# One kernel, its steps in another recorded order

## The chip, the core and the metric

The kernel runs on one core of a Trainium2 chip. TensorE (PE, with its weight loads PEld), VectorE (DVE), ScalarE (ACT) and GpSimd (POOL) each work through their own queue of instructions in order and wait for each other by semaphores; SyncE (SP) issues the DMAs, in order too. TensorE writes to PSUM only, and GpSimd is given SBUF operands alone in this kernel. The metric is the device time of one execution in microseconds.

## The reference

Attention with pooled queries, then a mixer of two layers over tokens and two over channels. B = 4, H = 8, S = 1152, D = 64; after pooling there are 576 queries; the mixer has 256 token units and 1536 channel units.

```python
def _attn_ref(q, k, v):
    q_pool = q.reshape(B, H, S // 2, 2, D).mean(axis=3)
    scores = scale * np.matmul(q_pool, k.transpose(0, 1, 3, 2))
    attn = np.exp(scores - np.max(scores, axis=-1, keepdims=True))
    attn = attn / (np.sum(attn, axis=-1, keepdims=True) + 1e-09)
    return np.matmul(attn, v)

def _moe_ref(x, w_tok1, w_tok2, w_ch1, w_ch2):
    xt = x.transpose(0, 2, 1)
    h = np.maximum(xt @ w_tok1, 0.0) @ w_tok2
    u = x + h.transpose(0, 2, 1)
    return u + np.maximum(u @ w_ch1, 0.0) @ w_ch2
```

q, k and v are float32; the weights are float64 and come as pairs of 32-bit words, which the kernel narrows on the chip (`narrow`, `tok_weights`).

## The kernel before

**Numbers.** A product of float32 is made of fast float32r products: each operand is split into a high part (a cast on ACT) and a low part (a subtraction, on DVE or GpSimd).

**Attention, 32 heads (`main`).** Per head nine steps; each fills one score tile (PSUM, `s`, two of them) with two blocks of 128 keys x 288 queries, by two matmuls each (L967). ACT takes two exponentials from the tile, `pf` (L981) and the high part `ph` (L984). A subtraction makes the low part `pl` (L988, on GpSimd or DVE). TensorE multiplies `ph` and `pl` by the values (L1015) into `o`. There are five `ph` and four `pl` buffers. In 17 heads (`IN_PV`) the values carry a column that gives the row sums, and a step has six such matmuls; in the others it has four, and DVE sums `pf` (L995).

**Ahead of a head.** `load_kq` and `prep_kq` load q and k for two heads, pool the queries (L731, L737), turn and split them. `stack` copies the parts by DMA into one of three sets `kk`, `qq` (L838) and into `k2`, `q2` (L843, L846); a set must have been read for the last time by the head three before. `maxima` multiplies queries by keys once more (L897) into one of three ring banks of PSUM (`r`), from which DVE reduces the row maximum (L899); the maxima go by DMA (L873) into a row of `q2`, so that the score matmul subtracts them.

**Beside it.** In head 1 `tok_weights` narrows the token weights: ACT takes absolute values (L659), GpSimd clamps them (L661, nine times), DVE puts the bits together, with two buffers `w`. After every fourth head `token_mix` runs the token layers for half of the channels (L1113, L1131). `finish` divides by the row sums (L1080 on ACT or L1081 on DVE).

**Channel mixer.** For each block of rows products by `w_ch1` (L1299, 384 columns) and `w_ch2` (L1416, 512 columns). Two thirds of the rows go in pairs, with seven products for eight (`paired`), for which weights are added (L1338) and all are split (L1288 on ACT, L1289 and L1402 on DVE or GpSimd). Sums are taken on DVE (L1370), the activation is split by ACT (L1307) and DVE (L1309). At the end rows of the mixer's input are loaded into one of three buffers (L1428), added (L1434) and stored (L1438, L1442).

**The order.** All this is written down as steps: an engine, the data and buffers it reads and writes, and for some of them a second engine (`other`: by `both` and `either`, and in `finish`). `Plan.run` takes the order of all 7279 steps from the string `ORDER` (differences of step numbers, packed), moves the steps listed in `OTHER` to their second engine, and issues them; a buffer of a pool goes to the step that comes first in this order. So the two tables decide each engine's queue and which buffer a step gets. `DUE` holds numbers that sorted the steps once; it does not change.

```python
order = [self.steps[n] for n in np.cumsum(near.T.copy().view("<i2")[:, 0])]
for n in OTHER:
    self.steps[n].eng, self.steps[n].cost = self.steps[n].other
```

Of the kernel before, what the change touches and what calls it, by code (L numbers as in the profile page):

```python
# [106 lines left out]
class Due(dict):  # L107
# [16 lines left out]
    "i8Sf1{lF*Bo8?fPXw@q}yaJ=+e2_{?3zit}3fxb;?`&yqQ!>+`#kt}Q_Qv)YIy&KW82h4=ATWbLSr>c%A(4sYGiA(qa2h>J}IKe8f*C2N>ms"
    "9bHg_RznZqi3YCXQ)~32|W_POO&lTy?^h9{Cmgsf|uBZ`rHe#uZfOUU$!wq{m|}{x<AZk-"
    ")<$;&>!X!L6Lzvcf$_8o=~SwYAI|*y96wwI)NPJ{#ch}B&(l?CI}(3X;~#^?jOoH7+d4^gG1PB|3ztW<E*PK<45d1gh{e;5|U?KTzBE=ju%s"
    "2Eo+xFY2KZY$ysz7&-"
    "GYzGIzYL!;y$>d^a&a9rd}xyTrog+^mkWpY@MGD%yHZe&NQ4<JD2ZYhh=6Zp|NEa%^_W)`R}u{jUpJG{W}jR)lm~pVSem1x9Pi4MfcWk6ZhS"
    "+SjJfite>6^RCWtt3jFRmbSBxH_l*xZMHQRb&2`<xfz?KWxBra4%~TJHZtONI%-"
    "<Qcb~pSx1_h(tNBT$?Ht37>z+R8eVXgcUBvwRmd%qMu)Q<Sxh&<rY`W^U=CBppU;1%uig4lX0r-q7>!jRI+X5EeJ-"  # L130
    "hZ)AOg=S+VL_a=83v^?2YH41<CshMCb_n__j?mW-JruPCyI8Z$ERn)!Q+A=9nb)_@wR8sl0(54pk;+tsNu<UTDiryS5n(`(XsO`4-u`J-"
    "NTwp+H|WFtujt(@?qems`P|THmWj3kF;opQJIn_QyD_w$Ec?Hwe{)uWTMH<X4*~gy!E^sBc=g{pzk@_QjSHN5uSIGqzeR*%rUVVXjDko^P^|"
    "%Va{efD5}euNB;?6n9iQ>giP4TsEH~mCZT3<hsxzU+z3XFOlzjY?VN-"
    "B|)#rJa2#9=O3ngj{_W=F)1sLar>0^)`5jXCzWkA^G`Dj{}yLB{pG4Cfm51I`OHl2KRfv@nW*oLz|ODsnXX@3<*19-"
    "hFMK&=~$rXnt=%O&vTlv!tb{3bV-bXf0A`My5jt$?W2>>P|28p%`r>PB_8lP%t1GnxqstU4qsz8_zk-8aB#cL0m+o-"
    "`fFN~R<)m6ZbIZto^$Hga7lIFonZ#(o8cesN0r+aUp>ffR)5FcdrkAZO*bEH;T4!BpdlyxT1FnmrVQl5U&R8=wF7*$ZLp)Q2dhMVIs5y~cDq"
    "xi`PB~ns3|M1GFklw6Adr6Iqu<+=@uQl|Mai2{^b*SQCs)7Pkz34^Q@Fj-$r*-"
    "+;_RPE8BVhKYE;co^D3F>tX4nv7CL5y__TVMn%gX=E0KHrIX=3PU9i<e>6w99Qbh-"
    "d**s%OQy%NSZOHXo5SA2Z{v69qIpho;vZd~q*}wy7WtZ2MMm3WCl5cdV(lQOobhrvsb3pbe=?F|CS87IMc^7)8F%58jzKQ#-"
    ";FrFz^wUP#EWpR$GN=wyQjp~KiP@F4HdoK1`o>W#V^YpOY}zbO+4Q<2znJQ%&N!DILNpw%N}{$)tOpm`M4v<a~XTe&9tlYmdy0Zns)bka?q7"  # L140
    "5kJ){q?{Gc61|FD4%=ZeozGw91RN4KjDVbiry{EatxktFu`j11ytZhzB(+=`kU(ScQFTQi`rezOYdb{feS0Y#Ud;m{+9z0@GcTnq7j%;P@fZ"
# [1410 lines left out]
```

## Time and profile before

| | us |
|---|---|
| runs | 857.30, 855.11, 857.35 (median 857.3) |
| profiled execution, span | 855.5 |
| PE busy | 831.3 |
| PEld busy | 770.9 |
| DVE busy | 737.9 |
| ACT busy | 589.4 |
| POOL busy | 508.3 |

The span runs from the first to the last instruction of the one execution that was profiled; it lies 1.8 us below the median of the runs. "Busy" is the time in which an engine had at least one instruction under way; of TensorE it says little, since its matmuls overlap. Attention with the token mixer takes the first 557 us or so, the channel mixer the rest. In rows of groups, the idle time behind the second bar is that of the engine ahead of these instructions, with what ended it.

### The profile page before, as it was taken

What the parts mean: (1) busy time and instruction counts of PE and PEld (TensorE: products, weight loads), DVE (VectorE), ACT (ScalarE), POOL (GpSimd) and SP (SyncE); (2) the same over time, 40 slices, a digit from 0 to 9 for tenths busy, and PEclk for the clock granted to TensorE, in tenths of its full rate; (3) what the DMA queues carried; (4) which work ended last, traced back from release to release, by engine and by line L of the source; (5) the groups of instructions that cost most, each with busy time, mean ns of one, the idle gap of its engine ahead of it and who ended that gap; (6) DMA issues with size and microseconds to landing.
All of it is one profiled execution on the core that took longest, in us unless ns stands there. A gap on an engine that the chain in (4) does not pass through costs nothing.

```text
span 855.5 us, 15871 instructions
## 1 busy us (share of the span) xinstructions
PE 831.3 (97%) x5282; PEld 770.9 (90%) x5282; DVE 737.9 (86%) x1537; ACT 589.4 (69%) x1222; POOL 508.3 (59%) x428
## 2 busy tenths in 40 slices
...
GB/s 185 251 136 141 153 137 152 159 132 148 140 154 149 129 142 161 167 149 154 130 136 141 95 143 86 61 197 173 123 149 38 107 64 24 1 62 86 1 1 112
DMA packets 252195, 104.15 MB, mean 122 GB/s; under 512 B 218640, under 2 KB 233104, under 8 KB 252112
## 3 DMA queue, kind: packets, MB, share of 16 engines
...
q8 instruction: 42, 0.69, 0.4%
...
## 4 chain that ended last, share of the span: by engine, by line
PE 75%; DVE 8%; ACT 5%; DMA 5%; SPq 3%; issue 2%; POOL 1%; DVEq 0%; ACTq 0%; POOLq 0%
PE r L1299 16%; PE o L1015 16%; PE s L967 12%; PE a L1416 11%; PE r L897 7%; PE r L1113 3%; PE r L1416 3%; PE o L1416 3%; PE r L1131 2%; ACT ph L984 2%; ACT pf L981 2%; DVE mx L899 2%; DMA qq<-qh 1%; DVE sum L995 1%; SPq L873 1%
## 5 line engine op out<-in xcount | busy, mean ns | idle before, releaser
L988 POOL TENSOR_TENSOR pl<-pf,ph 128x576 fp32r<-128x576 f32 x248 | 356.7, 1460 | 76.7 <-ACT pf L981 26.5
L981 ACT ACTIVATE pf<-s 128x576 f32<-128x576 f32 x288 | 191.7, 681 | 28.6 <-PE s L967 25.5
L1015 PE MATMUL o<-ph,vv 128*65 128x288 f32 (+2 forms) x882 | 205.5, 302 | 1.5 <-DVE ot L1028 0.8
L984 ACT ACTIVATE ph<-s 128x576 fp32r<-128x576 f32 x288 | 187.3, 658 | 25.6 <-PE s L967 9.4
L899 DVE TENSOR_REDUCE mx<-r 128x1 f32<-128x384 f32 x384 | 192.3, 547 | 14.0 <-PE r L897 11.8
L967 PE MATMUL s<-qq,kk 128*128 128x288 f32 x574 | 171.2, 306 | 4.6 <-ACT ph L984 3.5
L967 PE MATMUL s<-q,k 65*128 65x288 f32 x576 | 167.3, 299 | 0.4 <-DMA k<-kk 0.3
L1015 PE MATMUL o<-pl,vv 128*65 128x288 f32 (+1 forms) x576 | 149.5, 301 | 1.3 <-POOL pl L988 0.7
L1015 PEld LDWEIGHTS o<-ph,vv 128*65 128x65 f32 (+2 forms) x882 | 129.6, 154 | 6.8 <-DVE ot L1028 2.1
L897 PE MATMUL r<-kk,qq 128*128 128x384 f32 x372 | 126.8, 355 | 5.9 <-DMA qq<-qh 1.9
L967 PEld LDWEIGHTS s<-qq,kk 128*128 128x128 f32 x574 | 109.2, 190 | 11.2 <-ACT ph L984 6.7
L1416 PE MATMUL a<-big,h 128*128 128x512 f32 x432 | 113.4, 392 | 0.0
L967 PEld LDWEIGHTS s<-q,k 65*128 65x128 f32 x576 | 109.5, 190 | 0.9 <-issue 0.5
L995 DVE TENSOR_REDUCE sum<-pf 128x96 f32<-128x960 f32 x90 | 101.0, 1133 | 0.0
L1015 PEld LDWEIGHTS o<-pl,vv 128*65 128x65 f32 (+1 forms) x576 | 89.0, 162 | 3.9 <-POOL pl L988 1.0
L1416 PEld LDWEIGHTS a<-big,h 128*128 128x128 f32 x432 | 80.3, 188 | 12.8
L897 PEld LDWEIGHTS r<-kk,qq 128*128 128x128 f32 x372 | 70.1, 191 | 15.4 <-DVE mx L899 4.4
L1299 PE MATMUL r<-ut,wk 128*128 128x384 f32 x276 | 57.1, 339 | 0.0
L1289 POOL TENSOR_TENSOR wk<-wa,wk 128x256 fp32r<-128x256 f32 x19 | 15.0, 793 | 65.0 <-ACT wk L1288 64.9
L1299 PEld LDWEIGHTS r<-ut,wk 128*128 128x128 f32 x276 | 49.6, 188 | 3.1 <-issue 0.2
L1370 DVE TENSOR_TENSOR u<-r,u 128x384 f32<-128x384 f32 x59 | 32.4, 553 | 21.9 <-PE r L1299 20.8
L827 POOL TENSOR_TENSOR vv<-vn,vv 128x576 fp32r<-128x576 f32 x27 | 36.0, 1333 | 8.3 <-ACT vv L824 8.3
...
## 6 DMA issues: line engine op xcount, KB each, us to landing
...
```

Of the source, the lines that this page charges most:

```text
L827: both(NK * D, lambda e: e.tensor_sub(vv[:, :, lo], vn, f(vv)[:, :, hi]), t, ["vn", ("vv", h % 2)], [("vv", h % 2)])
L897: step(PE, mm(SP3), lambda ps=ps, w=w, x=x: te.matmul(at(ps)[:, 0:SP3], w, x, start=True, stop=True), t, read, [ps], [ps])
L899: step(DVE, dve(SP3), lambda ps=ps, m=m: ve.tensor_reduce(m, at(ps)[:, 0:SP3], axis=AX.X, op=ALU.max), t + due["max_of"], [ps], [key])
L967: te.matmul(at(st)[:, i, 0:HF], w[:, c * P:(c + 1) * P], x[:, fq * HF:(fq + 1) * HF], start=(n == 0), stop=(n == len(terms) - 1))
L981: step(ACT, act_ps(2 * HF) + (0 if near else 49), lambda pf=pf, st=st: sc.activation(pf, at(st)[:, :, 0:HF], AF.Exp, scale=ESC), t, [(st, ...
L984: step(ACT, act_ps(2 * HF) + 15, lambda ph=ph, st=st: sc.activation(at(ph), at(st)[:, :, 0:HF], AF.Exp, scale=ESC), t + due["p_hi"], [(st, ...
L988: both(2 * HF, lambda e, pf=pf, ph=ph, pl=pl: e.tensor_sub(at(pl), pf, f(at(ph))), t + due["p_lo"], [("pf", s), ph], [pl], [pl], on=POOL i ...
L995: step(DVE, 65 + 1.06 * (NK + 1) * HF // CUT, lambda fq=fq, cs=cs: ve.tensor_reduce(SUM[:, fq, cs], PF[:, 5 * fq:5 * fq + 5, cs].rearrange ...
L1015: lambda o=o, x=x, w=w, m=m, i=i, c=c, new=new, end=end: te.matmul(at(o)[0:m - w], VV[i2][:, c, w:m], at(x)[:, i], start=new, stop=end),
L1299: te.matmul(at(ps)[:, 0:GT], wb[:, u, c * P:(c + 1) * P], x[v_][:, c], start=(opens and c == 0 and n == 0), stop=(closes and c == H2 - 1 a ...
L1370: step(DVE, dve(GT), lambda: ve.tensor_add(at(out_), at(a)[:, 0:GT], at(b_)), t, [a, b_], [out_], [out_] if get else [])
L1416: te.matmul(at(ps), a[:, x * P:(x + 1) * P], b_, start=(opens and m == 0), stop=(closes and m == 2))
```

## The change

`ORDER` and `OTHER` get other values; nothing else changes. The steps, the work of each, what they depend on and the buffers are the same, 7279 in number. 224 steps change the engine: of the splits of the channel weights (L1289, L1402) 57 go from DVE to GpSimd and 16 the other way, of the weight sums 18 and 9, of the subtractions of `pl` 20 and 13, of the divisions in `finish` 36 from DVE to ACT and 20 back; the rest are smaller. Lines of the changed kernel stand 41 lower (L967 is L926 there, L1015 is L974, L661 is L620, L897 is L856, L1289 is L1248).

```diff
 ORDER = (
-    "c-n1Q1wa*B*PXacNvD9I5{j6Z*npIRhzg?EEnwm^z(B>qeu|<Ppdeu@h=pK_A_5W?-"
...
-OTHER = (20, 216, 218, 434, 435, 436, 437, 438, 619, 620, 621, 623, 632, 768, 769, 770, 772, 923,
+OTHER = (19, 20, 56, 434, 435, 436, 437, 438, 446, 619, 621, 632, 923, 934, 1007, 1480, 1481,
...
```

**TensorE, head 0 into head 1** (during the narrowing of the token weights). `s_82` and `s_83` are the two score tiles, `qq`/`kk` and `q`/`k` the operands of head 1's scores, `vv_119` the values of head 0. Before:

```order
L1015 MATMUL o<-pl_162,vv_119 65x288
L967 MATMUL s_82<-qq_96,kk_91 128x288
L967 MATMUL s_82<-q_99,k_94 128x288
L967 MATMUL s_82<-qq_96,kk_91 128x288
L967 MATMUL s_82<-q_99,k_94 128x288
L1015 MATMUL o<-ph_158,vv_119 64x288
L967 MATMUL s_82<-qq_96,kk_91 128x288
L967 MATMUL s_82<-q_99,k_94 128x288
L967 MATMUL s_82<-qq_96,kk_91 128x288
L967 MATMUL s_82<-q_99,k_94 128x288
L967 MATMUL s_83<-qq_96,kk_91 128x288
L967 MATMUL s_83<-q_99,k_94 128x288
```

and now:

```order
L926 MATMUL s_83<-q_99,k_94 128x288
L974 MATMUL o<-ph_155,vv_119 65x288
L974 MATMUL o<-ph_156,vv_119 64x288
L974 MATMUL o<-ph_155,vv_119 64x288
L974 MATMUL o<-ph_157,vv_119 65x288
L974 MATMUL o<-ph_155,vv_119 65x288
L974 MATMUL o<-pl_161,vv_119 65x288
L974 MATMUL o<-ph_157,vv_119 65x288
L926 MATMUL s_82<-qq_96,kk_91 128x288
L926 MATMUL s_82<-q_99,k_94 128x288
L926 MATMUL s_82<-qq_96,kk_91 128x288
L926 MATMUL s_82<-q_99,k_94 128x288
```

Before, a tile `s_82` is filled, one matmul of values follows, and `s_82` is filled again; now seven matmuls of values stand between the filling of `s_83` and that of `s_82`, and `s_82` was filled last 16 matmuls earlier.

**GpSimd, the clamping of the token weights** (`w_153`, `w_154`; `pl` are the subtractions of heads 0 and 1, `vv_120` the values of head 1). Before, from the first clamping on:

```order
L661 TENSOR_SCALAR w_153<-w_153 128x256
L661 TENSOR_SCALAR w_154<-w_154 128x256
L988 TENSOR_TENSOR pl_162<-pf,ph_156 128x576
L661 TENSOR_SCALAR w_153<-w_153 128x256
L661 TENSOR_SCALAR w_154<-w_154 128x256
L988 TENSOR_TENSOR pl_161<-pf,ph_158 128x576
L661 TENSOR_SCALAR w_153<-w_153 64x256
L661 TENSOR_SCALAR w_154<-w_154 128x288
L988 TENSOR_TENSOR pl_160<-pf,ph_155 128x576
L661 TENSOR_SCALAR w_153<-w_153 128x288
L661 TENSOR_SCALAR w_154<-w_154 128x288
L827 TENSOR_TENSOR vv_120<-vn,vv_120 128x9x64
```

and now:

```order
L620 TENSOR_SCALAR w_153<-w_153 128x256
L620 TENSOR_SCALAR w_154<-w_154 128x256
L620 TENSOR_SCALAR w_153<-w_153 128x256
L620 TENSOR_SCALAR w_154<-w_154 128x256
L947 TENSOR_TENSOR pl_161<-pf,ph_158 128x576
L620 TENSOR_SCALAR w_153<-w_153 64x256
L620 TENSOR_SCALAR w_154<-w_154 128x288
L620 TENSOR_SCALAR w_153<-w_153 128x288
L947 TENSOR_TENSOR pl_162<-pf,ph_159 128x576
L620 TENSOR_SCALAR w_154<-w_154 128x288
L786 TENSOR_TENSOR vv_120<-vn,vv_120 128x9x64
L620 TENSOR_SCALAR w_153<-w_153 128x288
```

The clampings stand closer together: four subtractions and one split of values lie between the first and the ninth before (the ninth is two rows further down), two subtractions and the split now.

**GpSimd, its last twelve instructions**, in the channel mixer (`wk`, `w2h`, `w2l` and `big` hold split weights, `ws` sums of weights, `wa` and `wb` the narrowed weights). Before:

```order
L1289 TENSOR_TENSOR wk_6915<-wa_6906,wk_6915 128x256
L1338 TENSOR_TENSOR ws_6920<-wa_6910 128x256
L1338 TENSOR_TENSOR ws_6921<-ws_6920,wa_6898 128x256
L1338 TENSOR_TENSOR ws_6923<-wa_6898,ws_6921 128x256
L1338 TENSOR_TENSOR ws_6922<-wa_6898,wa_6910 128x256
L1289 TENSOR_TENSOR w2h<-ws_6922,w2h 128x256
L1338 TENSOR_TENSOR ws_6921<-wa_6912 128x256
L1289 TENSOR_TENSOR wk_6915<-wa_6900,wk_6915 128x256
L1289 TENSOR_TENSOR wk_6919<-wa_6910,wk_6919 128x256
L1338 TENSOR_TENSOR ws_6921<-wa_6900,ws_6923 128x256
L1289 TENSOR_TENSOR wk_6914<-wa_6912,wk_6914 128x256
L1402 TENSOR_TENSOR big_71<-wb_6901,big_71 128x512
```

and now:

```order
L1248 TENSOR_TENSOR wk_6928<-wa_6917,wk_6928 128x256
L1361 TENSOR_TENSOR big_71<-wb_6904,big_70 128x512
L1248 TENSOR_TENSOR wk_6925<-wa_6907,wk_6925 128x256
L1248 TENSOR_TENSOR w2h<-ws_6930,w2h 128x256
L1297 TENSOR_TENSOR ws_6931<-wa_6907,ws_6929 128x256
L1297 TENSOR_TENSOR ws_6932<-wa_6909,ws_6930 128x256
L1248 TENSOR_TENSOR wk_6928<-wa_6919,wk_6928 128x256
L1297 TENSOR_TENSOR ws_6929<-wa_6909,wa_6921 128x256
L1248 TENSOR_TENSOR w2l<-ws_6929,w2l 128x256
L1361 TENSOR_TENSOR big_71<-wb_6906,big_70 128x512
L1248 TENSOR_TENSOR w2l<-ws_6931,w2l 128x256
L1361 TENSOR_TENSOR big_71<-wb_6908,big_70 128x512
```

Three splits of 512 columns stand among the last twelve now, where there was one. In the whole queue of GpSimd the splits of 256 columns go from 36 to 65, those of 512 columns from 4 to 16, the weight sums from 23 to 32.

## Rows read from the trace of the kernel before

**Rows 1.** The page, part 1, the engines: busy us, share, count.

```profile
PE 831.3 (97%) x5282; PEld 770.9 (90%) x5282; DVE 737.9 (86%) x1537; ACT 589.4 (69%) x1222; POOL 508.3 (59%) x428
```

**Rows 2.** Busy us per stretch of 20 us: PE, PEld, DVE, ACT, POOL; clock, DMA.

```profile
40.00:60.00 20.00, 16.25 (x74) 12.40 (x73) 18.32 (x44) 12.55 (x30) 19.04 (x17) 0.66 0.66 137
...
100.00:120.00 20.00, 19.64 (x138) 18.36 (x137) 19.68 (x47) 17.75 (x38) 18.34 (x17) 1.00 0.83 150
120.00:140.00 20.00, 19.77 (x148) 19.05 (x148) 19.37 (x40) 18.45 (x38) 19.28 (x15) 1.00 0.69 128
140.00:160.00 20.00, 17.56 (x118) 16.01 (x117) 18.08 (x36) 13.22 (x27) 15.88 (x13) 1.00 0.88 158
...
700.00:720.00 20.00, 20.00 (x102) 18.13 (x101) 14.34 (x26) 9.22 (x22) 9.35 (x11) 1.00 0.19 31
```

**Rows 3.** The chain that ended last: start, us, what, matmuls in it.

```profile
531.55 2.11 PE o L1015 x16
...
557.49 1.05 PE r L1299 x6
...
588.99 2.74 PE a L1416 x12
```

**Rows 4.** Groups by line: count, busy us, mean ns, idle us ahead.

```profile
L967 PE MATMUL s<-qq,kk 128*128 128x288 f32 x574 | 171.2, 306 | 4.6 <-ACT ph L984 3.5 <-ACT pf L981 0.9
...
L1299 PE MATMUL r<-ut,wk 128*128 128x384 f32 x276 | 57.1, 339 | 0.0
```

**Rows 5.** Timeline at 36 to 41 us, ACT and PE: start, us, instruction, [idle before].

```profile
36.34 0.63 ACT L984 ACTIVATE ph<-s 128x576 fp32r<-128x576 f32 x1
...
36.87 0.63 ACT L981 ACTIVATE pf<-s 128x576 f32<-128x576 f32 x1
...
40.08 0.65 ACT L984 ACTIVATE ph<-s 128x576 fp32r<-128x576 f32 x1
...
40.79 0.40 PE L967 MATMUL s<-qq,kk 128*128 128x288 f32 x1 [0.33 <-ACT ph L984]
```

**Rows 6.** Busy us per stretch of 2 us, columns as in rows 2.

```profile
52.00:54.00 2.00, 2.00 (x8) 1.39 (x7) 2.00 (x6) 0.75 (x3) 2.00 (x2) 0.50 0.02 4
...
58.00:60.00 2.00, 2.00 (x14) 1.72 (x13) 2.00 (x5) 0.69 (x2) 2.00 (x2) 1.00 0.62 96
```

**Rows 7.** The chain at 141 to 149 us.

```profile
143.29 5.33 DMA qq<-qh
...
148.75 0.42 PE r L897
```

**Rows 8.** Groups by line of the subtractions on GpSimd and DVE.

```profile
L988 POOL TENSOR_TENSOR pl<-pf,ph 128x576 fp32r<-128x576 f32 x248 | 356.7, 1460 | 76.7 <-ACT pf L981 26.5 <-ACT ph L984 24.3 <-PE o L1015 8.6
...
L1289 DVE TENSOR_TENSOR wk<-wa,wk 128x256 fp32r<-128x256 f32 x35 | 15.7, 456 | 3.3 <-ACT wk L1288 3.1
...
L1289 POOL TENSOR_TENSOR wk<-wa,wk 128x256 fp32r<-128x256 f32 x19 | 15.0, 793 | 65.0 <-ACT wk L1288 64.9
```

**Rows 9.** Timeline of GpSimd and DVE at 819 and 843 us.

```profile
819.23 1.01 POOL L1289 TENSOR_TENSOR wk<-wa,wk 128x256 fp32r<-128x256 f32 x1 [3.51 <-ACT wk L1288]
...
819.56 1.09 DVE L1309 SCALAR_TENSOR_TENSOR h<-u,h 128x384 fp32r<-128x384 f32 x1
...
843.41 0.55 DVE L1309 SCALAR_TENSOR_TENSOR h<-u,h 128x384 fp32r<-128x384 f32 x1
```

**Rows 10.** The chain at the end.

```profile
840.69 2.10 PE a L1416 x9
...
842.81 0.70 DVE u L1434
...
843.53 2.72 DMA out_dram<-u
...
846.63 3.59 DMA u<-mixed
...
851.00 0.69 DVE u L1434
```

More of the change, by code (lines that the diff above doesn't have):

```diff
@@ L124 @@
[L124 to L141, printed above, removed]
@@ new lines @@
+    "&a^9RTl`X`Ji0ZOq`<N&?c-@d)hQ($cP>-sm-T3v!ck0NkQhL4~|IJStRe;CVIu>n6jkX?P|Cq=o%hq@*b<ES4O;FH&NZ?46tvL-g1LwgLv%#b<u"
+    "5wWF9?d!#z$CghKup0xgw;eu;%C6SC{|7<19cU47%TQ!#m`!*`pS{eyY!20*u-C$vys#YOd+SH<%o~Xc9DWRXZjCJ{Jk3$s7&U+H9GV)L>k`iNFG"
+    "#^&Vc(=Du7G_ksGSn*Lg_Z31$@JNu@X3;2bsDCzih*9U%FZ7&v(M0u|JFja(y-d{JC^o2FV}$EkjadT31S*pvY(*CB`G;hjBC}i<@q-6bKP7A_AU"
+    "A5?Tst)V~W3#o-R2@i6Uag5v8bPh+y^{npsu26o^~7YMlGG@*JzDWWOWi!Y+^4<eCqFV^ap5gZ~I#0R4`jRLlC#AWHZeF(5q5V_n5$xBN=VHOSkn"
+    "6nM~<2@5gNQ3Am7X>uCh(5@`tR0PE!TLC?XAt?fCYJjnGB4@2u_Jcxz~p>B!jg9t?Njq>14)1KP0rif?PzxP{U^ZFW&QsgRF)gf9;=_j5bFE!BEz"
```

225 lines of the change are left out of this document (97 added, 128 removed), and 26 rows, old and new, of the table OTHER.

## The prediction

> **What bounds the kernel now.** I read the page first, then busy times by stretch, then the chain and the timelines at the thin places. The page calls TensorE (PE) busy for 97% of 855.5 us [rows 1], which says little, because matmuls overlap and a matmul that is held up counts as busy. So I count work by distance from start to start. Undisturbed stretches of the chain give 0.132 us for a matmul of 288 columns (2.11 for 16), 0.176 for 384 columns (1.05 for 6) and 0.229 for 512 (2.74 for 12) [rows 3].
>
> The attention stage runs until the first product of the channel mixer at 557.5 us [rows 3]. The code issues there 1154 score matmuls and 1458 of probabilities by values, 2612 x 0.132 = 345 us; 432 for the row maxima, 432 x 0.176 = 76 us; 464 of 256 columns in the token mixer, at an estimate of 0.176 x 256/384 = 0.117, 54 us; and transposes and warm-up matmuls, at an estimate of 24 us. That is 499 of 557: some **58 us** of PE's time are lost there. In the channel mixer, 792 x 0.176 + 648 x 0.229 = 288 us of work end at about 850, 293 us after they began; the first microseconds still hold attention work. No product waits [rows 4], and the table shows 20.00 us of 20 [rows 2]. **There is nothing to win behind 560 us, and something to lose.**
>
> Where the 58 us go: at 100 to 120 us PE, VectorE (DVE) and GpSimd (POOL) are all at 18.3 to 19.7 of 20; at 40 to 60 PE is at 16.25 and its granted clock at 0.66 of full, so it stood at the lower of its two levels (1.2 of 2.4 GHz) for a part of it; at 140 to 160 at 17.56 [rows 2]. At 40 to 60 four things meet: the splitting of the token weights loads GpSimd, ScalarE (ACT) and DVE, and the score tiles come too close to each other.
>
> **The change part by part.** No step comes or goes; 224 of those that may run on either of two engines change the engine, and each engine's queue is re-ordered. PE's work is the same, so the time can change only by waits.
>
> *Score tiles.* There are two in PSUM. A tile is free again when ACT has taken both exponentials from it: 0.53 us from the start of the first to the start of the second [rows 5], so about 1.09 for both with what ACT does in between added, plus 0.38 for the tails (matmul 0.306 instead of 0.132 in the mean of its group [rows 4], the exponential 0.65 instead of 0.53, 0.06 from its end at 40.73 to the matmul at 40.79 [rows 5]). For each of 288 re-uses I counted the PE work that stands between the last matmul into a tile and the first of its next tenant. Before, 26 re-uses have too little, by 12.4 us in all; the worst four stand in a row in head 1, with 0.13 to 1.33 us of work where 1.5 to 3.8 are wanted (the first piece shown of PE's order). The trace lost 22.9 us at these 26. After, 20 are short, by 4.2 us, none by over 0.7. Gain: between 0, where another queue is as late, and 22.9 x (1 - 4.2/12.4) = 15.1; at face value 8.2. I take **-10**, between the face value and what was really lost there, nearer to the first because GpSimd is full in this stretch too.
>
> *Banks of the maxima.* The same count for the three ring banks, each freed by DVE's reduction: short at 16 places by 2.7 us before, at 7 by 1.7 after. **-1** (0 to -4).
>
> *GpSimd at the weight split.* From its first subtraction to the ninth clamping of weights (second piece shown) GpSimd has one subtraction of 1.46 us for 576 columns [rows 8] less and one sum of queries of 256 columns less (an estimate of 1.46 x 256/576 = 0.65): 2.1 us. This lies under the same waits as the score tiles and is not added; it is why these can be won at all. If it were not so, the first term would shrink by that much.
>
> *The half clock.* PE's granted clock is 0.50 at 52 to 54, and with PE busy throughout, 8 matmuls start in 2 us; at 58 to 60, at 1.00, there are 14 [rows 6]. Before it fell, PE had waited again and again. The change shortens the waits but does not remove them: **0**, at best -3.
>
> *Keys and queries of the next head.* At 148.75 PE waits for a copy that took 5.33 us from its issue [rows 7], and whose issue had to wait for PE's last reading of the old copy. The PE work between this reading and the first maximum of the new head is 5.4 us before and 5.6 after in this head, so this wait stays. In heads 5, 7, 15 and 31 it falls by 0.8, 1.0, 0.9 and 1.2 us, from 7.4 to 9.8; there it is not the last wait now. SP's queue issues these copies in the order in which they stand, behind loads of q and k. **+1** (0 to +3.9).
>
> *Channel mixer.* GpSimd takes over some 64 steps more than it gives up there (splits L1289 36 to 65, weight sums L1338 23 to 32, splits L1402 4 to 16, L1283 2 to 14); the end of its queue shows it. A split costs 0.79 us there and 0.46 on DVE [rows 8]. What hides that is the lead of the split weights over their products; it is not shown by any row, except that PE never waits. But GpSimd also holds DVE up: a DVE instruction that began at 819.56, 0.33 us into a split on GpSimd, took 1.09 us, and one of the same line at 843.41, with GpSimd done, took 0.55 [rows 9]. I count 16 of this kind in the mixer, from 584.85 to this one, by 0.46 us in the mean; with twice the GpSimd work (my count: 107 us behind 53) they would be 32. DVE gives 27 us of work away and gets 7 us of hold-ups, so it is not the bound. **+1.5** (0 to the rival below).
>
> The Trainium skill, page "SBUF — State Buffer", section "Who interferes with whom", speaks against this part: a DVE instruction with two inputs in SBUF and a GpSimd instruction that reads SBUF exclude each other for the whole instruction. The row of 819.56 agrees (1.09 us instead of 0.55). By that rule every GpSimd step added also takes time from DVE, which is the third case below.
>
> *The tail.* In both, the last three output rows of a block need a load that waits for a store from the same buffer. Before: sum 0.70, store 2.72, 0.38 to the load, load 3.59, and the last sum began at 851.00 [rows 10], 0.7 us after PE, which had 42 matmuls left at 840.7 (42 x 0.229 = 9.6). After, 27 matmuls stand behind the last product, so PE ends 27 x 0.229 = 6.2 us after it. The last load waits for the store of a row that is done 3 products (0.53 us) ahead of that, so it lands 0.2 + 0.70 + 2.72 + 0.38 + 3.59 - 0.53 = 7.1 after it, 0.9 us after PE's end. **+0.2** (-0.5 to +1).
>
> Sum: -10 - 1 + 1 + 1.5 + 0.2 = **-8.3 us**, 855.5 - 8.3 = 847.2 of span. The median of the three runs (857.3) lies 1.8 above the profiled span, so 849.0 beside 857.3.
>
> **The rivals.** *The next queue is as late* (no change). At 100 to 140 us GpSimd is at 18.3 to 19.3 of 20 and DVE at 19.4 to 19.7 [rows 2], and through head 15 the two loads hardly change: my count gives DVE -0.8 us and GpSimd +2.4. Then a score tile freed earlier only waits for GpSimd's subtraction. Left is GpSimd's 2.1 us at the weight split, against it the 1, 1.5 and 0.2 of above: -2.1 + 2.7 = +0.6, so 857.9. Against it speaks that the worst places lie ahead of 60 us, where PE's wait names ACT's exponential [rows 5].
>
> *The mixer starves* (slower). Place: some 60 to 100 us into the channel mixer, where for 40 us of PE's work the new order gives GpSimd 13 us and DVE's steps with both inputs in SBUF 26 us by my count: 39 of 40, if the two exclude each other. Price: 29 splits dearer by 0.79 - 0.46 = 0.33, 9.6 us, and 16 more hold-ups of 0.46, 7.4 us; 17.0 if PE waited for all. It decides once a product stands less than about 1.3 us (0.79 split, 0.46 hold-up) behind the start of its split. With all of it, 849.0 - 1.5 + 17.0 = 864.5; with three quarters, 860. For it: the slack is not visible. Against it: PE does not wait once now, with the same kind of hold-up there [rows 2, 9].
>
> *More than counted*: score tiles at their 15.1, maxima 4, and the clock staying up for 3 gives -21 with the same costs, 838.
>
> **How the numbers follow.** A measurement of this kernel can tell about 0.3% from no change, that is 854.7 to 859.9. Forecast 849 with what lies around it (842 to 854.6): 0.55; more than counted (836 to 842): 0.08; no change: 0.17; the mixer starves: 0.20 (860 to 865). Faster 0.55 + 0.08 = 0.63, same 0.17, slower 0.20. The range leaves out 0.08 below 841 and some 0.10 above 863: 841 to 863. The forecast's own range is 842 to 854.6.
>
> **What would show it.** Right: in the stretch 36 to 56 us the waits of score matmuls for ACT fall below 1 us each, the first product of the channel mixer starts near 547, PE is at 20.00 of 20 behind it, and it ends some 0.9 us before the last sum. Head 9 still waits for its copy by 1 to 2 us. Wrong: the first product still starts at 555 to 558 (then the next queue was as late), or idle time ahead of L1299's counterpart in the mixer (then GpSimd starves it). What I cannot count is many small waits under 0.15 us, about 20 of the 58 us; if the new order makes these larger, the forecast falls without any place to point at.

## The result and the profile after

The changed kernel takes 848.28 us (median of 4 runs, 847.35 to 849.13) beside 857.19 for the one before: a ratio of 0.9907, 95% interval 0.9892 to 0.9922, 8.9 us faster. The profiled execution has a span of 847.4 us. Forecast were 849.0 for the median and 847.2 for the span. The sum was right; of its terms several were not, and they cancelled.

Part 1 of the page after, and busy time by stretch (columns as in [rows 2]):

```profile
PE 827.2 (98%) x5282; PEld 770.5 (91%) x5282; DVE 712.6 (84%) x1445; ACT 591.9 (70%) x1238; POOL 582.7 (69%) x504
```

```profile
40.00:60.00 20.00, 15.63 (x88) 13.22 (x88) 18.38 (x44) 13.39 (x33) 19.06 (x17) 0.83 0.77 157
...
140.00:160.00 20.00, 19.33 (x134) 17.77 (x133) 19.11 (x39) 15.67 (x32) 19.00 (x15) 1.00 0.67 116
...
700.00:720.00 20.00, 20.00 (x100) 17.89 (x99) 12.92 (x24) 7.00 (x16) 9.86 (x12) 1.00 0.20 46
```

GpSimd works 74 us more than before [rows 1], DVE 25 less. At 40 to 60 us GpSimd is as full as before (19.06 against 19.04, [rows 2]) and TensorE's share is no better; what is better is its granted clock, 0.83 of full instead of 0.66, and 88 of its matmuls start there instead of 74. At 140 to 160, where it lost most behind the weight split, TensorE goes from 17.56 to 19.33.

The chain of waits (start, us, what), once at the row that answers to 557.49 in [rows 3], and at the end, where it answers to [rows 10]:

```profile
550.00 1.05 PE r L1258 x6
...
841.21 1.37 PE r L1375 x6
842.58 0.02 issue
842.60 0.69 DVE u L1393
```

So the attention stage gained 557.49 - 550.00 = **7.5 us**. From there to the last sum it was 851.00 - 557.49 = 293.5 before and is 842.60 - 550.00 = 292.6 now, **0.9 less**. What follows the last sum grew by 0.3 (4.5 to 4.8). Together 8.1, the difference of the two spans.

Where in attention, I read by TensorE's own work, which is the same in all kernels here: the distances from start to start of its matmuls, less the pace of each kind (0.132 us for 288 columns, 0.175 for 384, 0.231 for 512, 0.119 for 256, the usual distance of each kind of transpose), summed over stretches of work. "20-40" is the work of the weight split; the first column holds the 1.4 us ahead of the first matmul as well. All kernels of the next sections are in the table; the numbers are us lost:

| | 0-20 | 20-40 | 40-100 | 100-120 | 120-320 | 320-360 | 360-500 | 500-780 | sum |
|---|---|---|---|---|---|---|---|---|---|
| before | 7.2 | 13.7 | 6.1 | 5.2 | 16.0 | 1.8 | 5.7 | 1.2 | 57.0 |
| after | 6.8 | 11.2 | 4.7 | 2.5 | 14.2 | 4.1 | 4.9 | 1.0 | 49.3 |
| head_new | 6.5 | 11.4 | 6.5 | 5.0 | 15.4 | 1.9 | 5.3 | 1.2 | 53.3 |
| head_old | 7.3 | 14.1 | 4.5 | 2.2 | 13.5 | 4.1 | 5.1 | 0.6 | 51.4 |
| mix_old | 6.6 | 10.9 | 5.1 | 2.4 | 14.0 | 3.1 | 4.9 | 1.1 | 48.1 |
| mix_pool | 6.5 | 11.9 | 4.4 | 2.4 | 14.8 | 3.5 | 5.0 | 33.2 | 81.9 |
| x_order | 7.8 | 11.5 | 5.4 | 2.4 | 34.5 | 9.4 | 28.0 | 28.6 | 127.7 |
| x_other | 7.6 | 14.2 | 7.1 | 5.2 | 19.5 | 2.7 | 12.4 | 7.4 | 76.0 |
| pl_back | 6.6 | 11.5 | 7.6 | 2.2 | 29.0 | 8.8 | 19.8 | 1.0 | 86.6 |
| pe_alone | 7.4 | 19.5 | 6.5 | 6.5 | 16.1 | 1.8 | 5.6 | 1.2 | 64.7 |
| v_early | 6.5 | 11.0 | 4.5 | 5.9 | 13.6 | 3.2 | 4.7 | 0.9 | 50.3 |
| copy9 | 7.4 | 14.3 | 5.9 | 10.3 | 16.2 | 1.8 | 5.0 | 1.2 | 62.3 |
| mend | 6.5 | 10.5 | 4.7 | 2.5 | 13.9 | 2.7 | 5.5 | 0.6 | 47.0 |
| mend2 | 6.5 | 11.7 | 5.2 | 2.1 | 14.0 | 1.9 | 5.5 | 0.6 | 47.5 |

Only 2.9 us of the gain lie in the first 40 us of work, though the four worst re-uses of score tiles are there; 4.1 lie at 40 to 120; and at 320 to 360 the new order loses 2.3 more than the old one (1.5, if a wait of 0.7 us that stands right at the border of 320 in the kernel before is counted behind it). At 100 to 120 the gain of 2.7 is not one of score tiles: before, TensorE waited there 0.65 us for a maximum and 0.31 and 1.48 us for two copies, now once, for 0.33 us.

### The profile page after: what moved, and what is told of

The parts are those of the page before. It is cut to its first block, busy times and chain, and to the rows that moved or that the text cites. A ratio compares the mean times of both kernels' runs of the same rounds, so it can differ in the third digit from the quotient of the medians.

```text
span 847.4 us, 15962 instructions
## 1 busy us (share of the span) xinstructions
PE 827.2 (98%) x5282; PEld 770.5 (91%) x5282; DVE 712.6 (84%) x1445; ACT 591.9 (70%) x1238; POOL 582.7 (69%) x504
## 4 chain that ended last, share of the span: by engine, by line
PE 76%; DVE 10%; DMA 4%; SPq 3%; ACT 3%; issue 2%; POOL 1%; DVEq 0%; ACTq 0%; POOLq 0%
PE r L1258 16%; PE o L974 16%; PE s L926 13%; PE a L1375 12%; PE r L856 7%; DVE mx L858 4%; PE r L1375 3%; PE o L1375 3%; PE r L1072 3%; PE r L1090 2%; DVE sum L954 2%; ACT ph L943 1%; DMA q<-mh 1%; DMA kn<-in_k_dram 1%; SPq L832 1%
## 5 line engine op out<-in xcount | busy, mean ns | idle before, releaser
L947 POOL TENSOR_TENSOR pl<-pf,ph 128x576 fp32r<-128x576 f32 x255 | 365.3, 1457 | 54.9 <-ACT pf L940 21.2
L974 PE MATMUL o<-ph,vv 128*64 128x288 f32 (+2 forms) x882 | 204.5, 303 | 3.8 <-ACT vv L783 2.5
L940 ACT ACTIVATE pf<-s 128x576 f32<-128x576 f32 x288 | 192.9, 682 | 20.3 <-PE s L926 15.4
L943 ACT ACTIVATE ph<-s 128x576 fp32r<-128x576 f32 x288 | 187.0, 658 | 21.2 <-PE s L926 10.5
L926 PE MATMUL s<-qq,kk 128*128 128x288 f32 x574 | 170.9, 307 | 1.5 <-ACT pf L940 1.0
L926 PE MATMUL s<-q,k 65*128 65x288 f32 x576 | 166.7, 299 | 0.6 <-issue 0.4
L974 PE MATMUL o<-pl,vv 128*65 128x288 f32 (+1 forms) x576 | 140.6, 298 | 0.3
L974 PEld LDWEIGHTS o<-ph,vv 128*64 128x64 f32 (+2 forms) x882 | 128.5, 153 | 9.7 <-ACT vv L783 2.7
L856 PE MATMUL r<-kk,qq 128*128 128x384 f32 x372 | 118.9, 347 | 4.4 <-issue 2.4
L926 PEld LDWEIGHTS s<-qq,kk 128*128 128x128 f32 x574 | 109.1, 190 | 7.0 <-ACT pf L940 2.4
L926 PEld LDWEIGHTS s<-q,k 65*128 65x128 f32 x576 | 109.4, 190 | 1.8 <-issue 0.8
L1375 PEld LDWEIGHTS a<-big,h 128*128 128x128 f32 x432 | 80.5, 188 | 13.6
L974 PEld LDWEIGHTS o<-pl,vv 128*65 128x65 f32 (+1 forms) x576 | 86.8, 161 | 2.9 <-DVE pl L947 0.4
L856 PEld LDWEIGHTS r<-kk,qq 128*128 128x128 f32 x372 | 68.3, 189 | 10.2 <-issue 2.5
L1248 POOL TENSOR_TENSOR wk<-wa,wk 128x256 fp32r<-128x256 f32 x34 | 28.5, 842 | 59.5 <-ACT wk L1247 59.5
L1247 ACT CAST wk<-wa 128x256 fp32r<-128x256 f32 x54 | 21.4, 404 | 40.0 <-PE r L1258 24.3
```

What stands on the lines that cost most here:

```text
L856: step(PE, mm(SP3), lambda ps=ps, w=w, x=x: te.matmul(at(ps)[:, 0:SP3], w, x, start=True, stop=True), t, read, [ps], [ps])
L926: te.matmul(at(st)[:, i, 0:HF], w[:, c * P:(c + 1) * P], x[:, fq * HF:(fq + 1) * HF], start=(n == 0), stop=(n == len(terms) - 1))
L940: step(ACT, act_ps(2 * HF) + (0 if near else 49), lambda pf=pf, st=st: sc.activation(pf, at(st)[:, :, 0:HF], AF.Exp, scale=ESC), t, [(st, ...
L943: step(ACT, act_ps(2 * HF) + 15, lambda ph=ph, st=st: sc.activation(at(ph), at(st)[:, :, 0:HF], AF.Exp, scale=ESC), t + due["p_hi"], [(st, ...
L947: both(2 * HF, lambda e, pf=pf, ph=ph, pl=pl: e.tensor_sub(at(pl), pf, f(at(ph))), t + due["p_lo"], [("pf", s), ph], [pl], [pl], on=POOL i ...
L974: lambda o=o, x=x, w=w, m=m, i=i, c=c, new=new, end=end: te.matmul(at(o)[0:m - w], VV[i2][:, c, w:m], at(x)[:, i], start=new, stop=end),
```

## Experiments: cutting the change in time

ORDER is one list, so the new order up to a point and the old one for all steps that are left is again a valid order. `head_new` has the new order for TensorE's first 40 us of work, `head_old` the old one there and the new one behind, `mix_old` the old one behind 499 us of work, where the channel mixer begins. Each step has the engine of the kernel whose order it is in. Here and below an edit of the two tables is written as the rule that makes them, since the tables themselves cannot be read.

```diff
-order = old
+first = new[:up to 40 us of TensorE's work]          # head_new; old and new swapped: head_old
+order = first + [n for n in old if n not in first]    # mix_old: up to 499 us
```

> All steps that the new order issues in TensorE's first 40 us of work (to about 59 us of the trace) in the new order and on the new engines; the rest in the order and on the engines of before. Theory (the two traces differ by 2.9 us at this point, and the rest of the gain lies behind it): 853.5 to 855.5. Rival (the whole gain comes out of the weight split, and what follows only shifts): 848 to 850.

Measured: 853.64 us, ratio 0.9951 (0.9936 to 0.9965), span 851.6. As the theory said: the first stretch brings 4.0 us by the medians and 3.0 by the first two columns of the table, and the rest lies behind it.

> The order and engines of before in TensorE's first 40 us of work (to about 62 us of the trace), then those of after. Theory (2.9 us of the gain lie ahead of this point and 5.2 behind it): 851 to 853. Rival (the whole gain comes out of the weight split): 856 to 858.

Measured: 851.02 us, ratio 0.9931 (0.9909 to 0.9953), span 849.3, as the theory said. Both parts together, 4.0 and 6.4, make 10.4 beside the 8.9 of the whole change; the interval of `head_old` alone is 3.8 us wide, so they add up as far as that can be told. The table shows each stretch with the losses of the order that it was given: 11.4 and 14.1 at 20 to 40, 1.9 and 4.1 at 320 to 360. In time, this change can be cut in pieces.

> The new order and engines up to TensorE's 499th us of work (about 549 us of the trace), then the order and engines of before: the channel mixer's part of the change is undone. Theory (the change does nothing in the mixer): 847.5 to 849.5. Rival A (giving GpSimd the splits costs, +1.5 us as forecast): 846 to 847.5. Rival B (it helps): over 850.

Measured: 848.79 us, ratio 0.9897 (0.9878 to 0.9917), span 846.2. As the theory said, but the interval is 3.3 us wide and would leave room for the +1.5 of the forecast. The traces decide: from 500 us of work on TensorE loses 1.2 us before, 1.0 with the change and 1.1 here. In the mixer the change costs TensorE nothing and gives it nothing.

## Experiments: order and engines apart

`x_order` has the new order with the old engines, `x_other` the old order with the new engines.

```diff
-OTHER = (19, 20, 56, 434, ...     # x_order: the new ORDER stays
+OTHER = (20, 216, 218, 434, ...   # x_other: the other way round
```

> The new order of all steps, but every step that has a second engine is on the engine of the kernel before (the 224 engine changes are undone). My account of the two traces: TensorE loses 56.8 us against its pace before and 49.1 after; 2.9 us of the gain lie in its first 40 us of work, 3.1 in the next 120, 1.5 in the rest of attention. Theory (the order beside TensorE's score tiles and banks brings the gain, the engine changes little): 848 to 851 us. Rival (the gain comes from the relief of DVE, which gave 92 instructions away): 855 to 858.

Measured: 933.0 us, ratio 1.086 (1.0829 to 1.0892).

> The order of before with the engines of after: the other half of the change alone. Theory (the order brings the gain): 855 to 859, no gain, perhaps a small loss, because a split costs 0.79 us on GpSimd where the order was made for 0.46 on DVE. Rival (relief of DVE): 849 to 852.

Measured: 875.41 us, ratio 1.0202 (1.0186 to 1.0217). Theory and rival fell in both. Half of the change with the other half undone costs 75 and 18 us. TensorE's longest waits (in all, times, longest) in `x_order`, and below in `x_other`:

```profile
PE o L1043 <- DVE pl L1016: 21.2, 13, 2.9
PE r L1327 <- DVE wk L1317: 11.8, 7, 5.4
```

```profile
PE o L1069 <- POOL pl L1042: 4.2, 6, 2.1
PE r L951 <- DVE mx L953: 4.2, 8, 0.9
```

Of what `x_order` loses more than the changed kernel, nearly all is behind 120 us of work (table). At the longest line TensorE waits for the very steps that changed engine: 12 of the 13 waits for `pl` on DVE are for subtractions that the changed kernel has on GpSimd, and DVE comes to them behind all that the order put there for it. In `x_other` the loss is spread over many short waits, and none of the six for `pl` on GpSimd is for a step that changed engine: these steps are on GpSimd in both kernels, and what changed is the rest of its queue. To see how few suffice, `pl_back` undoes only the engine changes of `pl`: 20 go back to DVE, 13 to GpSimd.

```diff
-OTHER = new
+OTHER = new, but old for the 33 steps L947 whose engine differs
```

> The new kernel with 33 of the 224 engine changes undone, those of the subtractions that make pl: 20 go back from GpSimd to DVE, 13 from DVE to GpSimd, at the places that the new order gives them. With all 224 undone the kernel took 933 us, and TensorE waited 21.2 us for 13 of these subtractions on DVE and 3.2 for one on GpSimd. Theory (a step's place in the order and its engine belong together, even for a few steps: DVE reaches a subtraction late where the order gave it to GpSimd): 866 to 880. Rival (it takes the weight of all changes together, some 35 us more on DVE): 849 to 855.

Measured: 881.99 us, ratio 1.0284 (1.0248 to 1.0319). The mechanism of the theory held, and the time lies 2 us above its range: 33 of 224 engine changes, given back, cost 34 us. It is not DVE's load: in number DVE gets 7 subtractions more, some 6 us at the 0.86 us that one takes in the mean in the kernel before. The waits, and DVE at the longest of them (TensorE went on at 392.01):

```profile
PE o L1046 <- DVE pl L1019: 19.2, 12, 2.9
```

```profile
389.23 1.01 DVE L930 TENSOR_REDUCE mx<-r 128x1 f32<-128x384 f32 x2
390.16 1.80 DVE L1019 TENSOR_TENSOR pl<-pf,ph 128x576 fp32r<-128x576 f32 x1
```

DVE has no gap ahead of the subtraction; it comes to it after two reductions of maxima, and then takes 1.80 us for it. So "the order" and "the engines" are not two causes with a share each. The gain belongs to the pair.

## Experiments: TensorE's queue alone, and the values of head 1

The largest term of the forecast was counted in TensorE's queue. `pe_alone` gives TensorE's queue the new order at the weight split and leaves all other queues as before. The edit in TensorE's queue begins so:

```diff
-MATMUL o<-ph_157,vv_119 65x288
-MATMUL o<-pl_161,vv_119 65x288
-MATMUL o<-ph_156,vv_119 65x288
-MATMUL r_76<-kh,qd_102 128x384
-MATMUL o<-ph_157,vv_119 64x288
-MATMUL o<-pl_160,vv_119 65x288
 MATMUL s_82<-qq_96,kk_91 128x288
```

> The kernel before with one change: in TensorE's work from 24 to 40 us (the weight split beside heads 0 and 1) TensorE's queue alone stands in the new order; ACT, DVE, GpSimd and the DMA queue keep the order of before. The four worst re-uses of score tiles lie here; before, 8.7 us were lost at them. Theory (TensorE's queue is what makes the tiles late): 851 to 854. Rival (the queues behind it are as late: ACT, DVE and GpSimd must follow in the same order or nothing is won): 856 to 860.

Measured: 864.08 us, ratio 1.0073 (1.0054 to 1.0091): slower than before. The theory fell, and the time lies above the rival's range too. TensorE's two longest waits at 36 to 60 us:

```profile
PE r L1099 <- DVE w2l L726: 3.9, 1, 3.9
PE o L1065 <- POOL pl L1038: 2.9, 2, 2.7
```

Of the waits of score matmuls for ACT one is left (1.2 us), and TensorE waits for DVE's narrowing and GpSimd's subtractions instead. Here the distance between two uses of a tile in TensorE's queue is worth something only if the other queues deliver in that order.

TensorE's waits at 36 to 56 us, in the kernel before and then in the changed one:

```profile
PE s L967 <- ACT ph L984: 2.9, 4, 1.2
PE r L897 <- DVE w2l L676: 1.1, 1, 1.1
PE o L1015 <- POOL pl L988: 0.7, 1, 0.7
PE r L1049 <- DVE w2l L676: 0.5, 1, 0.5
PE o L1015 <- POOL vv L827: 0.4, 1, 0.4
```

```profile
PE o L974 <- ACT vv L783: 2.5, 1, 2.5
PE r L1008 <- DVE big L635: 1.2, 1, 1.2
PE s L926 <- ACT pf L940: 0.9, 1, 0.9
PE o L974 <- POOL vv L786: 0.7, 1, 0.7
```

The waits for the tiles have shrunk from 2.9 to 0.9 us, but all waits together only from 5.6 to 5.3. The longest one is new, the cast of head 1's values, and the last, their split on GpSimd, has grown from 0.4 to 0.7. Their load is issued at 35.16 (at 26.39 before), and lands 6.9 us later, and their cast on ACT begins at 44.38. `v_early` puts the load (DMA queue), the cast (ACT) and the split (GpSimd) ahead, shown in this order:

```diff
 DMA u_64<-in_moe_w_tok_dram 128x1152 x2
+DMA vn<-in_v_dram 128x9x64
 DMA qn<-in_q_dram 128x4x128 x2
 DMA qq_97<-qh_116 64x576
 DMA q_98<-mh 1x64x1
-DMA vn<-in_v_dram 128x9x64
...
 ACTIVATE w_154<-u_64 128x288
+CAST vv_120<-vn 128x9x64
 ACTIVATE ph_156<-s_82 128x576
...
 ACTIVATE u_63<-r_77,rd_128 128x64
-CAST vv_120<-vn 128x9x64
...
 TENSOR_SCALAR w_154<-w_154 128x288
+TENSOR_TENSOR vv_120<-vn,vv_120 128x9x64
 TENSOR_SCALAR w_153<-w_153 128x288
 TENSOR_TENSOR pl_162<-pf,ph_159 128x576
 TENSOR_SCALAR w_154<-w_154 128x288
-TENSOR_TENSOR vv_120<-vn,vv_120 128x9x64
```

> The new order with three steps moved: the load of head 1's values goes ahead of the point where it stood by some 8 us (where it stood in the kernel before), their cast on ACT and their split on GpSimd go ahead by some 4 us. After the change TensorE waits there 2.5 us for this cast and 0.7 for the split, and its granted clock falls to 0.50 from 45 to 51 us. Theory (this wait is what took back a part of the gain at the score tiles): 842 to 845.5, of which 3.2 us are the waits and up to 3.2 the half clock. Rival (GpSimd is full there, 19.06 of 20 us, so that the next thing TensorE waits for is GpSimd's subtractions): 847 to 849.

Measured: 849.36 us, ratio 0.9898 (0.988 to 0.9917), span 848.4. The theory fell. The mechanism of the rival held, with another engine than it named: the wait for the values is gone, and these are the longest at 36 to 56 us now:

```profile
PE o L1046 <- ACT ph L1015: 2.3, 1, 2.3
PE r L1080 <- DVE big L707: 1.1, 1, 1.1
```

All waits there come to 5.7 us, and the work of the weight split loses 11.0 us instead of 11.2: the wait has moved from one queue to the next. The time lies 0.4 us above the rival's range; at 100 to 120 this kernel loses 5.9 instead of 2.5, because head 9's copy comes late there again (see below), and behind it the clock is at 0.50 for a while (mean 0.91 at 140 to 160 us).

## Experiments: the mixer with more on GpSimd

`mix_pool` moves to GpSimd all 104 steps of the mixer that could be on either engine and were still on DVE.

```diff
-OTHER = new
+OTHER = new, but GpSimd for every step of L1242, L1223 to L1232, L1248, L1297, L1361
```

> The new order, with all 104 steps of the channel mixer that could be on either engine and are on DVE (43 splits of 256 columns, 20 of 512, 25 splits of 384 and 16 weight sums) moved to GpSimd: some 93 us more for GpSimd by the cost table, nearly twice what the change itself gave it there. Theory (the weights are split so far ahead that the mixer does not starve): 848 to 850. Rival (the mixer starves): each of the 63 weight splits is at least 0.33 us dearer, and they come in the order made for DVE; 858 to 880.

Measured: 881.15 us, ratio 1.0264 (1.022 to 1.0309). The theory fell, the rival held, with a time 1 us above its range. TensorE's longest waits, and a stretch of the mixer (columns as in [rows 2]):

```profile
PE r L1337 <- POOL wk L1327: 8.9, 8, 2.9
PE a L1454 <- POOL big L1440: 5.4, 3, 2.9
```

```profile
720.00:760.00 40.00, 34.17 (x138) 29.43 (x137) 12.88 (x23) 15.25 (x35) 31.26 (x35) 0.83 0.22 55
```

GpSimd is at 31.26 of 40 there, DVE at 12.88, and TensorE waits, and the clock goes with it. So the rival *the mixer starves* names something that can happen, and the change stays short of it; but what TensorE waits for at its longest lines is GpSimd's own splits, not a step of DVE that they hold up. How DVE pays for work on GpSimd shows in the line with both inputs in SBUF (groups by line of the kernel after, then of `mix_pool`; mean ns behind the comma):

```profile
L1268 DVE SCALAR_TENSOR_TENSOR h<-u,h 128x384 fp32r<-128x384 f32 x37 | 24.1, 668 | 3.9 <-ACT h L1266 3.8
L1248 POOL TENSOR_TENSOR wk<-wa,wk 128x256 fp32r<-128x256 f32 x34 | 28.5, 842 | 59.5 <-ACT wk L1247 59.5
```

```profile
L1347 DVE SCALAR_TENSOR_TENSOR h<-u,h 128x384 fp32r<-128x384 f32 x37 | 28.9, 798 | 20.5 <-ACT h L1345 20.4
L1408 DVE TENSOR_TENSOR u<-r,u 128x384 f32<-128x384 f32 x59 | 32.3, 553 | 68.7 <-PE r L1337 68.5
```

The line of the kernel before took 624 ns; 668 becomes 798, while the line that has one input in PSUM takes 553 in all three kernels, with the heaviest load on GpSimd too. The Trainium skill, page "SBUF — State Buffer", section "Who interferes with whom", says that a DVE instruction with two inputs in SBUF contends with GpSimd's reads and one with a single such input does not; both rows agree.

## Experiments: the queue of DMAs

Before, TensorE waited for head 9's copy [rows 7]. `copy9` is the kernel before with four loads moved from ahead of these copies to behind them:

```diff
-DMA qn<-in_q_dram 32x18x32
 DMA qd_102<-qh_116 64x64
-DMA qn<-in_q_dram 32x18x32
 DMA q_99<-mh 1x128x1
-DMA kn<-in_k_dram 32x36x32
-DMA qn<-in_q_dram 32x18x32
 DMA qd_102<-qh_116 64x64
 DMA k_94<-kk_91 64x1152
 DMA kk_90<-kh 64x1152
 DMA kk_90<-kl 64x1152
 DMA qq_95<-qh_115 64x576 x2
-DMA qn<-in_q_dram 32x18x32 x3
+DMA qn<-in_q_dram 32x18x32 x2
+DMA kn<-in_k_dram 32x36x32
+DMA qn<-in_q_dram 32x18x32 x4
```

> The kernel before with four steps moved: four loads of q and k (three of 72 KB, one of 144 KB) that are issued from 135.3 to 138.6 us, ahead of head 9's copies, go behind these in the DMA queue. Before, the last copy took 5.33 us to land (4.80 us after the change) and TensorE waited 1.64 us for it; at this stretch (TensorE's work from 100 to 120 us) it loses 5.12 us before and 2.43 after the change. Theory (the copies land late because these loads are in flight with them): the copy lands in 4.3 to 4.8 us, the wait falls below 0.9, the stretch to 4.0 to 4.5; 856 to 857 in all, near the limit of what can be measured. Rival (how long a copy takes has to do with the other copies, not with these loads): 5.1 to 5.4 us, and the stretch keeps its 5.1.

Measured: 862.24 us, ratio 1.0052 (1.0034 to 1.007): 4.8 us slower. The theory fell: the two copies of the queries land in 4.3 and 5.3 us (4.8 and 5.3 before), the last one as the rival said, so the four loads are not what makes it slow. The trace of the kernel before could have shown it: the four loads had landed by 141.35, and the copies of the queries were issued at 141.92 and 143.29. What the trace does show is that the four copies of head 9 land one behind the other, in the order of their issue (before at 144.58, 145.84, 146.73 and 148.61); that fits the rival, but no run tests it. The stretch did not keep its 5.1 us, it lost 10.3, and whether the wait itself shrinks can't be read, because a longer one came ahead of it (GpSimd, then TensorE's wait):

```profile
149.89 1.54 POOL L782 TENSOR_TENSOR qp<-qn 128x192 f32<-128x192 f32 x2 [6.78 <-DMA qn<-in_q_dram]
```

```profile
152.87 0.61 PE L1066 MATMUL o<-pl,vv 128*128 128x288 f32 x1 [6.18 <-POOL pl L1039]
```

A sum of queries on GpSimd waits for one of the loads that I moved, and the subtractions behind it in GpSimd's queue wait with it: loads that no one on TensorE needs for long held TensorE for 6 us.

In the changed kernel the copies of head 9 land sooner (tile `qq`, issue to landing), and at 320 to 360 us of work two new waits stand, shown with what stands ahead of them on DVE and in the DMA queue:

```profile
DMA to landing us min/median/max: 4.2/4.5/4.8
```

```profile
363.18 1.82 DVE L690 TENSOR_TENSOR qp<-qn 128x384 f32<-128x384 f32 x1
...
365.64 0.45 PE L856 MATMUL r<-kk,qq 128*128 128x384 f32 x1 [1.09 <-DVE mh L828]
```

```profile
380.43 0.59 SPq L797 DMA_DIRECT2D qq<-qh  x1
381.12 0.54 SPq L797 DMA_DIRECT2D kk<-kl  x1
...
386.19 0.54 SPq L797 DMA_DIRECT2D kk<-kh  x1
...
390.20 0.41 PE L856 MATMUL r<-kk,qq 128*128 128x384 f32 x1 [1.70 <-issue]
```

`mend` moves the sum to GpSimd and head 24's last copy to the others:

```diff
 DMA kk_90<-kl 64x1152
+DMA kk_90<-kh 64x1152
 DMA q_99<-mh 1x128x1
 DMA q_99<-mh 1x64x1
 DMA qn<-in_q_dram 32x18x32
 DMA q_98<-mh 1x64x1
 DMA kn<-in_k_dram 32x36x32
-DMA kk_90<-kh 64x1152
```

> The new kernel with two steps mended, at the two places where its trace loses more than the one of before. First: head 24's copy of the high part of the keys, which the new order issues 5 us behind the other three copies of this head (386.19 against 380.43 and 381.12), while TensorE waits 1.70 us at 390.20 for the product that reads it; it goes right behind the others. Second: a sum of queries on DVE between two reductions of row maxima, which took 1.82 us beside a subtraction on GpSimd while TensorE waited 1.25 us at 365.64; it goes to GpSimd, behind the subtraction that ends at 366.27, where GpSimd idles for 1.05 us. Theory (both waits are caused by these places alone): -1.9 and -1.25, 845 to 846.5, with 0.3 to 0.6 lost in TensorE's work from 320 to 360 us instead of 4.1. Rival (the next queue is as late there too): 847.5 to 849.

Measured: 847.41 us, ratio 0.9878 (0.9862 to 0.9895), span 845.0. Both waits are gone, but the stretch loses 2.7 us, not 0.3 to 0.6: of the 3.5 to 3.8 us that the theory wanted back, 1.4 came. The time lies between the two expectations. One of the waits that took their place, and the copy it is for:

```profile
386.61 0.37 PE L998 MATMUL s<-q,k 65*128 65x288 f32 x1 [1.02 <-DMA q<-mh]
```

```profile
383.82 0.51 SPq L906 DMA_DIRECT2D q<-mh  x1
```

The maxima that this copy carries were ready at 363.3 in this kernel (the 365.7 of the next expectation is from the trace of the changed one). `mend2` puts it ahead of the others:

```diff
 DMA q_98<-mh 1x128x1
+DMA q_98<-mh 1x64x1
 DMA kn<-in_k_dram 32x36x32
...
-DMA kk_90<-kh 64x1152
 DMA q_99<-mh 1x128x1
 DMA q_99<-mh 1x64x1
+DMA kk_90<-kh 64x1152
 DMA qn<-in_q_dram 32x18x32
-DMA q_98<-mh 1x64x1
```

> The mended kernel with two more moves in the DMA queue. There TensorE, which came to this place earlier, waited 1.02 us at 386.61 for a row of maxima of head 22; the data of this copy were ready at 365.7, but it stood in the DMA queue behind head 24's copies and a load of q and was issued at 383.82. It goes ahead of them now (beside the issue at about 377), and head 24's copy of the keys goes behind the two copies of maxima that follow. Theory (the place in the DMA queue alone makes this wait): TensorE's work from 340 to 360 us loses 0.2 to 0.5 us instead of 1.54 (2.52 in the new kernel, 0.24 in the one before), 843.5 to 844.5 of span beside 845.0 of the mended kernel. Rival (the next queue is as late): 1.2 to 1.6 us in this stretch, 845 of span.

Measured: 847.15 us, ratio 0.9877 (0.9861 to 0.9894), span 845.5. The wait is gone, 320 to 360 loses 1.9 us as in the kernel before, and at 340 to 360 it is about 0.9, between the two expectations. The span did not follow: at 20 to 40, where nothing was changed, 1.2 us more were lost than in `mend`. By their ratios both mended kernels lie 0.3% below the change, with intervals that touch its own; they were not timed against each other, and I don't call them faster.

## Why the prediction was right, and where its steps were not

| term | forecast | measured |
|---|---|---|
| attention: score tiles -10, maxima -1, half clock 0, copies +1 | -10 | -7.5 |
| mixer, up to the last matmul | +1.5 | -0.2 |
| from the last matmul to the last sum | +0.2 | -0.7 |
| what follows | 0 | +0.3 |
| sum | -8.3 | -8.1 |

**Score tiles.** The step that was mis-sized. The 22.9 us that the prediction weighed were lost in all the work between two fillings of a tile, whatever TensorE waited for there. The waits of score matmuls for ACT, which a tile freed earlier would end, are these in all of the kernel before, and in all of the changed one:

```profile
PE s L967 <- ACT ph L984: 3.5, 6, 1.2
PE s L967 <- ACT pf L981: 0.9, 3, 0.4
```

```profile
PE s L926 <- ACT pf L940: 1.0, 2, 0.9
PE s L926 <- ACT ph L943: 0.3, 1, 0.3
```

By the distances at these places it is 6.0 us before and 1.8 now: some **4 us** of gain instead of 10. Counted at the 20 re-uses of the kernel before with less than 1.47 us of work between them, 18.5 us were lost in these pieces of work, and only 5.9 of it right ahead of the tile's next matmul; the rest was other waits and half clock. At the weight split the case *the next queue is as late* was the true one for the waits: 5.6 us of them became 5.3, and `v_early` shows the next wait behind the one removed. The prediction had written this down ("if it were not so, the first term would shrink"). That the 2.9 us gained in the first 40 us of work are near the 2.1 by which GpSimd's queue was reckoned shorter is chance, as the next paragraph shows. And the prediction has no term for the place where head 1's values are loaded and cast, although they stand in the same queues.

**Half clock.** Forecast 0, at best -3; it was a large part of the gain. TensorE's granted clock stands at the lower level (0.50, 1.2 of 2.4 GHz) for a shorter time:

```profile
48.00:50.00 2.00, 2.00 (x9) 1.86 (x8) 1.73 (x5) 1.14 (x2) 2.00 (x4) 0.50 0.76 180
...
52.00:54.00 2.00, 2.00 (x14) 1.66 (x13) 2.00 (x6) 1.19 (x2) 2.00 (x3) 1.00 1.14 216
```

At 52 to 54 us it is back at 1.00, where [rows 6] has 0.50. A mean of 0.66 over 20 us is 13.6 us at 0.50, and 0.83 is 6.8. The matmuls that started at 0.50 and that no wait of over 0.15 us followed took 4.7 us more than their pace before and 2.2 now: some **2.5 us** of gain, which is most of the 2.9 in the first 40 us of work. The new order goes with this: at 40 to 60 us the mean is 0.57 to 0.66 in the four kernels that have the old order of all queues at the weight split, and 0.74 to 0.83 in the nine that have the new one there (`v_early` but for three steps). It also differs between executions with one order: 0.83 in the kernel after, `head_new`, `mix_old` and `mend`, which lose 11.2, 11.4, 10.9 and 10.5 us at 20 to 40, and 0.74 in `mix_pool` and `mend2`, which lose 11.9 and 11.7.

**Small waits.** The prediction could not count them. All distances longer than the pace that belong neither to a wait of over 0.15 us nor to the half clock come to 29.6 us before and 29.8 now, so they did not move.

**Copies.** +1, and it was some +0.5: 1.15 us less at head 9, 1.7 more at head 24. But not one place was right. Head 9 did not keep its wait: 1.48 us before, 0.33 after, with the second copy landing in 4.8 us instead of 5.33 [rows 7]. In `v_early`, with the same row of DMAs there, it took 5.8 us again and TensorE waited 1.90, so this part of the gain depends on more than the order. Heads 5, 7 and 31 show no wait; one of 0.31 us in head 15 is for a maximum on DVE. The new one is head 24's, and the count could not see it: it measures TensorE's work between the last reading and the first product, not where the copy stands in the DMA queue.

**Mixer and tail.** +1.5 was not there; `mix_old` gives the same time. The splits did get dearer (0.79 to 0.84 us on GpSimd) and DVE's instructions longer (0.62 to 0.67), as reckoned, but TensorE waited for none of it. The tail was +0.2 by a store of 2.72 and a load of 3.59 us; here the last load took as long (3.5 us), but the store ahead of it took 1.8, so that the load had landed at 842.2, ahead of TensorE's end, and the last sum began 0.02 us behind it.

Of the signs named ahead, TensorE at 20.00 of 20 in the mixer and waits of score matmuls for ACT below 1 us (0.9) came; the first product of the mixer at 547 (550.00), an end of TensorE 0.9 us ahead of the last sum (0.02) and a wait of 1 to 2 us in head 9 (0.33) did not. Some sums of the prediction are wrong by themselves: with 15.1, 4 and 3 us of gain and the same costs, *more than counted* is -19.4, not -21 (its 838 goes with -19.4); the tails of a tile's re-use add up to 0.35 us, not 0.38; and by [rows 3] the paces of 384 and 512 columns are 0.175 and 0.228. They matter little for the forecast.

So the exact total is luck: attention brought 2.5 us less than forecast, what follows took 2.3 less, and inside attention the tiles brought less than half of their term while a term put at 0 brought 2.5. The sign and the range rested on less: a mixer that TensorE fills to 20.00 of 20 before and after, and an attention stage in which the waits for score tiles did shrink. There the direction was right, and its reasons in part.
